# A new order of steps in a hand-written plan: the scaled up-projection weights used as they arrive, and steps moved between ScalarE, VectorE and GpSimd

## The chip, the cores and the metric

The kernel runs on one core of a Trainium2 chip. The metric is the device time of one execution in microseconds (us). Of three executions of the kernel before, the median was 151.3 us (148.43 to 152.84). A profiled execution took 148.72 us, and its span from the first to the last profiled instruction is 146.9 us. The engines are called by the names that the profile uses: PE is TensorE (PEld its weight loads), DVE is VectorE, ACT is ScalarE, POOL is GpSimd, and SP is SyncE, which here only issues transfers.

## The reference

A linear attention with a decaying state (batch 4, 8 heads, 768 positions, head size 48) is followed by a layer norm, a two-layer MLP with ReLU, and a residual:

```python
for t in range(S):
    cur = np.einsum('bhd,bhe->bhde', u[None] * kt, vt)
    y[:, :, t] = np.einsum('bhd,bhde->bhe', rt, state + cur)
    state = w[None, :, :, None] * state + np.einsum('bhd,bhe->bhde', kt, vt)
...
x = np.ascontiguousarray(attn_out.transpose(0, 2, 1, 3)).reshape(B, S, H * D)
...
xn = (x - mu) / np.sqrt(var + 1e-06) * g_ln
ch = np.maximum(xn @ w_ch1, 0.0) @ w_ch2
return (x + ch).astype(np.float32)
```

The model width is 8 x 48 = 384, the hidden width 1536.

## The kernel before

The 4 x 768 positions are cut into 24 chunks of 128, six to a sequence. Two chunks form a pair (12 pairs). For the MLP the chunks are put in 18 groups: groups 0 to 7 have one chunk each, 8 to 13 two, 14 to 17 one.

Every piece of work is a small function, a *step*, called by its name, a number and an engine letter: `v` for DVE, `s` for ACT, `g` for POOL, and `-` where the engine is fixed (PE for products, SP for transfers). The string `PLAN` (line 18 on) lists 755 such steps, and the last loop of the kernel calls them in that order. Nothing reorders them afterwards: on each engine the steps run in the order of the list, each held back only by waits for the data it reads and for the buffers it overwrites. So a step that waits holds all later steps of its engine. SP's transfers use eight completion semaphores in turn, so an issue there also waits for the landing of the transfer eight places before it.

The steps that matter here:

- `LK`, `LR2`/`LR`, `LV`: SP loads k, r and v of a chunk or a pair. `SK` and `SR2`/`SR` scale k and r by powers of the decay to bf16 (line 205). `TDk` turns a pair of scaled k by a transposing transfer (line 423); `TRr` turns r on PE and `TCr` copies it out of PSUM.
- `Q2` multiplies the turned k and r of a pair (line 205). `AT` forms the scores of a chunk on PE (line 544), `AM` masks them on DVE (line 553).
- `S` forms the chunk's own part of the state and the diagonal sums on PE (lines 460, 481); `ZU` and `ZD` carry the state on (ZD is a product by line 205), `CC2` copies the diagonal sums and `VB2` multiplies them by v (line 492).
- `Y` adds up the attention output on PE (lines 575, 583). `S` and `Y` share one PSUM bank, so `S` of a later pair waits until DVE's `X` (line 590) has read the `Y` before it. `X` writes the chunk's x and its row sums.
- `SQ` and `RS` make the norm's factor (RS on ACT in lines 613 and 614, on POOL in 616 and 619), `XN` the centred x in bf16. `LT` and `XT` (on PE and a copy), or from group 8 on the transposing transfer `LTD` (line 623), turn it.
- `LW1,n` loads a third of w1 as float; `SW,3n+kc` scales a piece of it into bf16 (line 342 on ACT, 344 on DVE, 346 on POOL). `IW2,n` loads a third of w2 (POOL's own transfers).
- `UP,16g+m` forms 512 columns of the hidden layer of group g on PE (line 646). For a group of one chunk, m = 0, 1, 2 uses the third 0, 1, 2 of w1. `RL` with the same number is the ReLU out of PSUM (662 on ACT, 664 on DVE). Two PSUM banks serve UP: an UP waits for the RL of the UP whose bank it takes.
- `DN,4i+d` adds a third of the down-projection of chunk i on PE (line 674), into a single bank; `OT` (line 730) multiplies by `RS` and adds x, and must have read the bank before the next chunk's `DN` starts. `STO` stores.
- `DU` are products with zeros that keep PE running in the first part (line 279).

Of the kernel before, what the change touches and what calls it, by code (L numbers as in the profile page):

```python
# [28 lines left out]
SW,1,s VB2,2,g AT,7,- AM,6,v LK,9,- Y,4,- RL,34,s UP,0,- IW2,1,g X,4,v UP,18,- RL,0,s AM,7,v IW2,2,g Y,5,- XN,4,s LT,3,- UP,32,-
RL,18,s RS,1,g LV,8,- X,5,v LT,4,- UP,33,- RL,32,s XT,3,v XN,5,g DU,512,- CV2,3,v LV,9,- UP,16,- RL,33,s XT,4,v SK,8,v S,6,-  # L30
DN,0,- SR2,4,v CC2,3,s RL,16,s UP,48,- SQ,5,s ZU,6,v UP,64,- VB2,3,v RL,48,s TRr,4,- SQ,3,s Y,6,- SK,9,g DN,1,- RS,3,s X,6,v
RL,64,s UP,66,- RS,0,g TDk,4,- SQ,2,s DN,2,- RS,2,g LT,5,- S,7,- OT,0,v RL,66,s UP,49,- XN,6,s XT,5,v UP,50,- RL,49,v TCr,4,s
LR2,6,- DN,4,- ZU,7,v DN,5,- UP,80,- ZD,7,v LK,10,- CV2,4,g RL,50,v Y,7,- RL,80,s X,7,v LV,13,- DN,6,- Q2,4,v XN,7,s UP,65,-
SQ,4,s OT,1,v LV,11,- AT,8,- SQ,6,s SR2,6,v AT,9,- DN,8,- RS,6,s LR2,5,- AM,8,v RS,4,s DN,9,- SQ,7,s LK,11,- S,8,- DN,10,-
ZU,8,v LV,10,- UP,82,- CC2,4,s OT,2,v VB2,4,g LK,12,- LT,6,- AM,9,v Y,8,- RL,82,s DN,12,- STO,0,- RL,65,s SK,10,g DN,13,- XT,6,v
LK,13,- X,8,v DN,14,- ZD,8,g LV,12,- S,9,- UP,96,- OT,3,v SK,11,g ZU,9,v UP,98,- RL,96,s SR2,5,v Y,9,- TDk,5,- SQ,8,s DN,16,-
CV2,5,v LT,7,- TRr,5,- SK,12,v DN,17,- X,9,v TCr,5,s RL,98,v LK,15,- UP,97,- XN,9,g LK,14,- XT,7,v ZD,9,g UP,81,- RL,97,s
LR2,7,- XN,8,s SK,13,g UP,112,- RL,81,s LTD,8,- DN,18,- RS,7,s Q2,5,v TRr,6,- OT,4,v UP,114,- SK,15,g TCr,6,s RL,112,v STO,1,-
S,10,- CV2,6,g DN,20,- CC2,5,s TDk,6,- RL,114,s SK,14,v AT,10,- RS,5,s AT,11,- ZU,10,v DN,21,- SR2,7,g AM,10,v UP,113,- STO,3,-
DN,22,- AM,11,v RL,113,s TDk,7,- Y,10,- VB2,5,g UP,129,- OT,5,v TRr,7,- RL,129,s LR,19,- UP,130,- ZD,10,g X,10,v UP,133,-  # L40
LV,14,- Q2,6,v RL,130,s DN,24,- TCr,7,v STO,2,- S,12,- DN,25,- CC2,6,s LV,15,- XN,10,s VB2,6,g ZU,12,v AT,12,- SQ,9,s AT,13,-
STO,5,- AM,12,v Y,11,- RL,133,s DN,26,- Q2,7,g LK,16,- X,11,v UP,128,- OT,6,v XN,11,s Y,12,- UP,131,- X,12,v LK,17,- DN,28,-
AM,13,v SR,19,g CV2,7,s S,13,- DN,29,- LTD,9,- ZU,13,v SQ,12,s DN,30,- ZD,13,g RL,128,s Y,13,- OT,7,v AT,15,- SQ,11,s LR2,8,-
AT,14,- X,13,v UP,132,- STO,4,- SK,17,g RL,131,v SQ,13,s LR,18,- S,14,- AM,15,v LV,17,- XN,13,s DN,32,- LV,16,- XN,12,s DN,33,-
ZU,14,v RL,132,s SK,16,v UP,144,- CC2,7,v AM,14,v LTD,10,- VB2,7,g UP,147,- RL,144,s DN,34,- SQ,10,s SR2,8,v TDk,8,- Y,14,-
RS,8,s UP,145,- RL,147,s OT,8,v UP,148,- TRr,8,- ZD,14,v TCr,8,s RL,145,v X,14,v RL,148,v DN,36,- LK,18,- DN,37,- CV2,8,v
XN,14,s S,15,- UP,149,- ZU,15,v LK,19,- UP,161,- ZD,15,g RL,149,v LV,18,- DN,38,- RL,161,s Q2,8,v STO,7,- Y,15,- LV,20,-
UP,146,- SK,18,g X,15,v STO,6,- AT,16,- RL,146,s AT,17,- XN,15,v LR,20,- UP,164,- RS,9,g OT,9,v LTD,11,- AM,17,v UP,160,-
RL,164,s RS,10,g DN,40,- RL,160,v S,16,- SK,19,v UP,163,- SR,18,v CC2,8,s TDk,9,- UP,165,- ZU,16,v RL,163,s AM,16,v DN,41,-
ZD,16,g RL,165,s DN,42,- VB2,8,g LR,21,- UP,162,- OT,10,v TDr,9,- Y,16,- RL,162,v DN,44,- X,16,v DN,45,- XN,16,g UP,176,-  # L50
LV,19,- SR,20,g DN,46,- RL,176,s STO,8,- Y,17,- OT,11,v UP,178,- LK,20,- X,17,v DN,48,- Q2,9,v LK,21,- UP,177,- XN,17,g SR,21,v
DN,49,- LTD,12,- RL,177,s RL,178,v DN,50,- CV2,9,v AT,19,- OT,12,v AT,18,- SK,20,g STO,9,- UP,180,- AM,18,v STO,11,- S,18,-
SK,21,g RL,180,s UP,181,- CC2,9,v ZU,18,v DN,52,- VB2,9,g AM,19,v RL,181,s STO,10,- UP,179,- SQ,16,s TDk,10,- DN,53,- RL,179,s
# [4 lines left out]
SR,22,v S,20,- RL,210,v UP,212,- TDr,11,- CC2,10,v DN,65,- SK,22,v VB2,10,g ZU,20,v DN,66,- Y,20,- TDk,11,- OT,16,v UP,209,-
X,20,v DN,68,- RL,209,s ZD,20,v STO,14,- S,21,- XN,20,g RL,212,v CV2,11,s DN,69,- LTD,14,- ZU,21,v SQ,20,s DN,70,- UP,213,-
RS,13,s OT,17,v STO,16,- UP,211,- STO,15,- Y,21,- RL,211,s DN,72,- X,21,v DN,73,- Q2,11,v SQ,21,s AT,23,- ZD,21,v RL,213,s  # L60
AT,22,- XN,21,v S,22,- LTD,15,- UP,224,- ZU,22,v AM,22,v DN,74,- ZD,22,g RL,224,s UP,226,- CC2,11,s RS,14,s OT,18,v VB2,11,g
# [721 lines left out]
```

## Time and profile before

| | us |
|---|---|
| three executions, median (lowest, highest) | 151.3 (148.43, 152.84) |
| profiled execution, its own time | 148.72 |
| its span | 146.9 |
| PE busy in the span | 140.5 |
| DVE, ACT, POOL busy | 110.7, 82.4, 71.8 |

The time lies 1.8 us above the span, for what comes before the first and after the last instruction. PE's busy time is modelled from pipelined matmuls, so it is read beside the idle time and the starts of the instructions. The granted TensorE clock was full in the whole span.

### The profile page before, as it was taken

The numbers are of one execution on the slowest core, as the hardware profiler recorded it, in microseconds if no ns is written. First come the engines' busy times: TensorE is split into PE (matmuls) and PEld (weight loads), VectorE is DVE, ScalarE is ACT, GpSimd is POOL, SyncE is SP. The second block draws the span as 40 slices with busy tenths as digits, with TensorE's granted clock in tenths as the row PEclk, the third lists the DMA queues.
The fourth block names the chain that finished last, engine by engine and source line by source line (L and its number), as shares of the span: only waits on it lengthen the run. The fifth ranks groups of instructions, "written<-read, shape, count | busy, mean of one in ns | idle before, by whom it ended". The sixth has DMA issues, their size and how long they took to land.

```text
span 146.9 us, 4689 instructions
## 1 busy us (share of the span) xinstructions
PE 140.5 (96%) x1943; PEld 111.1 (76%) x1943; DVE 110.7 (75%) x206; ACT 82.4 (56%) x181; POOL 71.8 (49%) x96
## 2 busy tenths in 40 slices
...
GB/s 114 285 251 265 182 373 161 287 230 213 220 90 235 199 229 153 219 204 262 218 192 196 178 216 170 185 206 225 204 103 198 175 119 173 84 49 115 11 97 110
DMA packets 85097, 27.18 MB, mean 185 GB/s; under 512 B 80338, under 2 KB 83540, under 8 KB 85076
## 3 DMA queue, kind: packets, MB, share of 16 engines
...
q8 instruction: 15, 0.25, 0.7%
...
HBM read 18.88 MB, written 4.72 MB: 161 GB/s over the span
## 4 chain that ended last, share of the span: by engine, by line
PE 78%; SPq 10%; DMA 6%; ACT 1%; issue 1%; DVE 1%; POOL 1%
PE hp L646 32%; PE o L674 31%; DMA w_f<-in_moe_w_ch_dram 6%; SPq L352 4%; PE at L544 3%; PE y L583 3%; SPq L374 2%; PE y L575 2%; PE y L481 2%; SPq L371 2%; PE at L400 2%; PE y L460 1%; SPq L377 1%; ACT w_sb L342 1%; SPq L218 1%
## 5 line engine op out<-in xcount | busy, mean ns | idle before, releaser
L646 PE MATMUL hp<-xT,w_sb 128*128 128x128 bf16 (+1 forms) x648 | 56.9, 238 | 0.7 <-ACT w_sb L342 0.7
L662 ACT ACTIVATE hT<-hp 128x512 bf16<-128x512 f32 x55 | 32.3, 594 | 41.4 <-PE hp L646 40.7
L674 PE MATMUL o<-w_sb,hT 128*128 128x384 bf16 x276 | 53.1, 326 | 0.5 <-DVE ot L730 0.5
L646 PEld LDWEIGHTS <-w_sb 128*128 128x128 bf16 x648 | 49.4, 114 | 4.8 <-ACT w_sb L342 1.2
L674 PEld LDWEIGHTS <-hT 128*128 128x128 bf16 x276 | 25.0, 97 | 12.6 <-issue 0.6
L553 DVE TENSOR_TENSOR A<-at,mask 128x1024 bf16<-128x1024 f32 x20 | 24.1, 1216 | 1.6 <-PE at L544 1.5
L730 DVE SCALAR_TENSOR_TENSOR ot<-o,rs,x 128x384 f32<-128x384 f32 x23 | 14.1, 615 | 12.8 <-PE o L674 7.0
L492 POOL TENSOR_TENSOR Vb<-vf,cc 128x768 f32<-128x768 f32 x11 | 16.5, 1499 | 14.7 <-ACT cc L200 7.8
L205 POOL TENSOR_TENSOR sk<-kf,Fk 128x384 bf16<-128x384 f32 x13 | 13.7, 1063 | 9.1 <-DMA kf<-in_k_dram 8.4
L597 ACT ACTIVATE sqj<-x,sm 128x384 bf16<-128x384 f32 x24 | 14.6, 610 | 2.2 <-DVE x L590 2.2
L205 POOL TENSOR_TENSOR Z<-ZS,WLZ 128x384 bf16<-128x384 f32 x8 | 8.0, 1001 | 15.3 <-DVE ZS L565 15.3
L590 DVE SCALAR_TENSOR_TENSOR x<-y,Vb 128x384 f32<-128x384 f32 x20 | 11.0, 552 | 4.8 <-PE y L583 3.7
L664 DVE TENSOR_SCALAR hT<-hp 128x512 bf16<-128x512 f32 x17 | 11.5, 682 | 3.3 <-PE hp L646 3.3
L279 PE MATMUL o<-warm 128*128 128x512 bf16 x33 | 11.3, 427 | 1.0 <-DVE warm L228 1.0
L200 ACT COPY trr<-at 128x512 bf16<-128x512 bf16 (+1 forms) x13 | 9.1, 762 | 5.1 <-PE at L400 5.1
L205 DVE TENSOR_TENSOR sr<-rf,Fr 128x768 bf16<-128x768 f32 (+1 forms) x11 | 9.3, 855 | 2.0 <-DMA rf<-in_r_dram 2.0
L205 POOL TENSOR_TENSOR sr<-rf,Fr 128x384 bf16<-128x384 f32 (+1 forms) x5 | 6.6, 1326 | 6.8 <-DMA rf<-in_r_dram 6.8
L205 DVE TENSOR_TENSOR q<-trk,trr 128x1024 bf16<-128x1024 bf16 x9 | 7.5, 833 | 1.6 <-DMA trk<-sk 1.3
L604 ACT ACTIVATE xn<-x,sm 128x384 bf16<-128x384 f32 x13 | 7.8, 610 | 1.3 <-DVE x L590 1.3
L606 POOL TENSOR_SCALAR xn<-x,sm 128x384 bf16<-128x384 f32 x8 | 4.9, 614 | 7.1 <-DVE x L590 7.0
L481 PE MATMUL y<-vv,sk 128*128 128x96 bf16 (+1 forms) x96 | 7.4, 205 | 0.0
L583 PE MATMUL y<-vv,A 128*128 128x48 bf16 x160 | 7.2, 183 | 0.0
...
## 6 DMA issues: line engine op xcount, KB each, us to landing
...
rf<-in_r_dram SPq DMA_DIRECT2D x9, 384.0 KB, 5.0
...
w_sb<-in_moe_w_ch_dram POOLq DMA_DIRECT2D x3, 384.0 KB, 6.5
...
kf<-in_k_dram SPq DMA_DIRECT2D x2, 384.0 KB, 4.6
```

What stands on the lines that cost most here:

```text
L205: engines[e].tensor_tensor(out=out, in0=in0, in1=in1, op=ALU.mult)
L279: nc.tensor.matmul(out=warm_ps[0][:].rearrange("p (a t) -> p a t", a=4), lhsT=warm[:], rhs=rhs, start=True, stop=True)
L492: engines[e].tensor_tensor(out=Vb2(g).rearrange("p (x h d) -> p x h d", x=2, h=H), in0=vals, in1=cc2(g)[:].unsqueeze(3).to_broadcast([P, 2 ...
L553: nc.vector.tensor_tensor(out=AA(i)[:].rearrange("p e q t -> p (e q) t"), in0=psum["at", i][:].rearrange("p e q t -> p (e q) t"), in1=mask ...
L583: nc.tensor.matmul(out=t[:, h * D : (h + 1) * D], lhsT=AA(i)[:, par, q, :], rhs=vv(i)[:, h, :], start=first, stop=True, skip_group_check=True,
L590: nc.vector.scalar_tensor_tensor(out=xx(i)[:], in0=psum["y", i][:, :C], scalar=1.0, in1=Vb(i), op0=ALU.mult, op1=ALU.add, accum_out=sm[i][:],)
L597: nc.scalar.activation(out=sqj[:], in_=xx(i)[:], func=ACT.Square, bias=sm[i][:], scale=-float(C), accum_out=sq[g][:, j : j + 1])
L646: nc.tensor.matmul(out=t[:, a * gw : (a + 1) * gw], lhsT=w1_sb[n][kc][:, fb::FB], rhs=xT(g)[:, :size, kc, :], start=(kc == 0), stop=(kc == ...
L662: nc.scalar.activation(out=o, in_=s, func=ACT.Relu)
L664: nc.vector.tensor_relu(out=o, in_=s)
L674: nc.tensor.matmul(out=psum["o", i][:, :C], lhsT=hT(g)[:, fk, j * P : (j + 1) * P], rhs=w2_sb[d][:, a, :], start=(fk == 0), stop=(fk == FK ...
L730: nc.vector.scalar_tensor_tensor(out=ot(i)[:], in0=psum["o", i][:, :C], scalar=rs[g][:, j : j + 1], in1=xx(i)[:], op0=ALU.mult, op1=ALU.add,)
```

## The change

Only `PLAN` changes, from the eighth line of its list on. The same 755 steps with the same numbers are called. SP's 110 steps stand in the same order. On PE some 38 of 255 steps stand elsewhere. 45 steps go to another engine, among them `SW,8` (ACT to POOL), `SW,0` (DVE to POOL), `RS,1` and `RS,2` (POOL to ACT), `Q2,3` and `VB2,4` (POOL to DVE), `Q2,5`, `SR2,5`, `SK,8`, `SK,12` (DVE to POOL), and 13 `RL` between ACT and DVE. Two lines of the table:

```diff
-XT,0,v Y2,3,- SW,7,s TCk,3,v X,2,v SW,8,s AT,5,- AT,4,- X,3,v XN,2,g DU,512,- UP,2,- AM,5,v XN,3,s IW2,0,g LV,7,- UP,1,- RL,2,s
+Y2,3,- TCk,3,v SW,7,s X,2,v X,3,v SW,6,s RS,1,s XN,2,s AT,5,- AT,4,- DU,512,- UP,1,- SW,8,g AM,5,v CV2,2,v UP,2,- LT,2,-
...
```

The first place is the start of the up-projection on PE. `w1_sb1` and `w1_sb2` are the scaled thirds 1 and 2 of w1; `hp` is the PSUM bank, `xT0` the turned chunk 0. Before:

```order
L279 MATMUL o_256<-warm_202 128x512
L646 LDWEIGHTS w1_sb2_0_232
L646 MATMUL hp_799<-xT0_129,w1_sb2_0_232 128x128
L646 LDWEIGHTS w1_sb2_1_233
L646 MATMUL hp_799<-xT0_129,w1_sb2_1_233 128x128
L646 LDWEIGHTS w1_sb2_2_234
L646 MATMUL hp_799<-xT0_129,w1_sb2_2_234 128x128
```

and in the changed kernel:

```order
L279 MATMUL o_256<-warm_202 128x512
L646 LDWEIGHTS w1_sb1_0_229
L646 MATMUL hp_800<-xT0_129,w1_sb1_0_229 128x128
L646 LDWEIGHTS w1_sb1_1_230
L646 MATMUL hp_800<-xT0_129,w1_sb1_1_230 128x128
L646 LDWEIGHTS w1_sb1_2_231
L646 MATMUL hp_800<-xT0_129,w1_sb1_2_231 128x128
```

`UP,1` (third 1) moves ahead of `UP,2` (third 2). On POOL the piece of third 2 with kc = 2 (`SW,8`) now follows `Q2,2`.

The second place is POOL after the last load of w2: `rs0` to `rs2` are `RS,0` to `RS,2`, `xn2` is `XN,5`, and `sk1_83` is written by `SK,9` before and by `SK,8` and `SK,9` after.

```order
 L349 DMA w2_sb2_237<-in_moe_w_ch2_dram 128x1536
-L616 TENSOR_SCALAR rs1_185<-sq1_166 128x1
-L619 TENSOR_TENSOR rs1_185<-rs1_185,expo_206 128x1
-L606 TENSOR_SCALAR xn2_128<-x5_119,sm5_146 128x384
-L205 TENSOR_TENSOR sk1_83<-kf0_69,Fk_213 128x8x48
 L616 TENSOR_SCALAR rs0_184<-sq0_165 128x1
 L619 TENSOR_TENSOR rs0_184<-rs0_184,expo_206 128x1
-L616 TENSOR_SCALAR rs2_186<-sq2_167 128x1
-L619 TENSOR_TENSOR rs2_186<-rs2_186,expo_206 128x1
+L205 TENSOR_TENSOR sk1_83<-kf0_69,Fk_213 128x8x48 x2
```

`RS,0` stood behind `SK,9` and now stands ahead of it.

The third place is POOL just after that: `sr2_87` is `SR2,5`, `sk2_84` is `SK,10` and `SK,11` (`SK,11` first after the change), `Z0` and `Z1` are `ZD,8` and `ZD,9`, the first `sk0_82` is `SK,12`, `q1_98` is `Q2,5`, and the last row is `SK,13`.

```order
 L202 CAST vv1_89<-vf4_81 128x768
-L492 TENSOR_TENSOR Vb0_112<-vf4_81,cc1_103 128x768
-L205 TENSOR_TENSOR sk2_84<-kf1_70,Fk_213 128x8x48
+L205 TENSOR_TENSOR sr2_87<-rf1_74,Fr2_209 128x16x48
+L205 TENSOR_TENSOR sk2_84<-kf1_70,Fk_213 128x8x48 x2
 L205 TENSOR_TENSOR Z0_105<-ZS2_111,WLZ_221 128x384
-L205 TENSOR_TENSOR sk2_84<-kf1_70,Fk_213 128x8x48
-L606 TENSOR_SCALAR xn2_128<-x9_123,sm9_150 128x384
+L205 TENSOR_TENSOR sk0_82<-kf2_71,Fk_213 128x8x48
 L205 TENSOR_TENSOR Z1_106<-ZS0_109,WLZ_221 128x384
+L205 TENSOR_TENSOR q1_98<-trk2_93,trr2_96 128x1024
 L205 TENSOR_TENSOR sk0_82<-kf2_71,Fk_213 128x8x48
```

`VB2,4` and `XN,9` leave POOL; `SR2,5`, `SK,12` and `Q2,5` come in, all ahead of `SK,13`, which `TDk,6` on SP waits for.

More of the change, by code (lines that the diff above doesn't have):

```diff
@@ L29 @@
[L29 to L53, printed above, removed]
@@ L58 @@
[L58 to L61, printed above, removed]
@@ new lines @@
+RL,34,s RL,18,s LV,8,- LV,9,- UP,0,- XN,4,s RL,0,s UP,32,- SK,9,g CV2,4,g TDk,4,- LR2,6,- LK,10,- LV,13,- LV,11,- LR2,5,-
+LK,11,- SR2,5,g SK,11,g SK,10,g LT,4,- UP,33,- DU,512,- Q2,3,v CV2,3,v XT,4,v RL,32,s RL,33,s UP,16,- UP,50,- RL,50,s DN,0,-
+S,6,- CC2,3,s SQ,5,s UP,48,- RL,48,s SQ,3,s RS,3,s XN,5,v SR2,4,v ZU,6,v TRr,4,- Y,6,- DN,1,- UP,66,- LT,5,- DN,2,- VB2,3,v
+X,6,v RL,16,v S,7,- UP,49,- OT,0,v XT,5,v RL,49,v ZU,7,v ZD,7,v DN,4,- DN,5,- SQ,2,s RL,66,s XN,6,s UP,64,- UP,80,- RL,64,s
+TCr,4,s Y,7,- DN,6,- X,7,v OT,1,v Q2,4,v UP,65,- AT,8,- AT,9,- AM,8,v LV,10,- LK,12,- STO,0,- LK,13,- LV,12,- TDk,5,- DN,8,-
```

46 lines of the change are left out of this document (35 added, 11 removed).

## The prediction

> **What bounds the kernel now.** First the stage from 45 to 90 us of the span (its length, then busy us of PE, PEld, DVE, ACT, POOL with their instructions, the clock granted, the DMA share, GB/s):
>
> ```profile
> 45.00:90.00 45.00, 45.00 (x609) 36.93 (x607) 41.22 (x73) 26.83 (x65) 25.39 (x24) 1.00 1.04 210
> ```
>
> From 45 us on PE has no idle time, at the full clock: there order can win nothing, only lose. What can be won lies earlier. The chain of waits shows where (start, length, engine, what is written and line):
>
> ```profile
> 24.71 0.86 ACT w_sb L342 x2
> 25.57 0.39 issue
> 25.96 0.71 ACT w_sb L342
> ...
> 40.81 0.61 ACT hT L662
> 41.42 0.20 POOL rs L616
> 41.69 0.56 POOL rs L619
> 42.28 0.63 DVE ot L730
> ```
>
> Two places: the scaling of w1 on ACT releases the first UP piece by piece, and RS,0 on POOL holds OT,0, for which DN,4 waits. PE's rows there, from the timeline (start, length, engine, line, what it writes from what, count, and in brackets the idle time before it and who ended that):
>
> ```profile
> 25.49 0.25 PE L646 MATMUL hp<-xT,w_sb 128*128 128x128 bf16 x1
> 26.11 0.25 PE L646 MATMUL hp<-xT,w_sb 128*128 128x128 bf16 x1 [0.37 <-ACT w_sb L342]
> 26.72 1.42 PE L646 MATMUL hp<-xT,w_sb 128*128 128x128 bf16 x22 [0.36 <-ACT w_sb L342]
> 27.98 0.33 PE L631 MATMUL at<-ident,xn 128*128 128x128 bf16 x3
> ...
> 40.95 1.50 PE L646 MATMUL hp<-xT,w_sb 128*128 128x128 bf16 x24
> 42.95 1.46 PE L674 MATMUL o<-w_sb,hT 128*128 128x384 bf16 x8 [0.49 <-DVE ot L730]
> ```
>
> From 26.72 to 27.98, 22 products take 1.26 us, so 0.057 us each and 0.68 for an UP of 12; a busy pair of UP (24) at 40.95 would end at 42.3, and DN,4 starts at 42.95: 0.65 lost. At 25.49 two products of 0.057 were spread over 1.23 us: 1.1 lost.
>
> **Front: UP,1 first, SW,8 on POOL.** The scaling of w1 in the timeline of POOL and ACT, with Q2,2 between (the second row), and the weight loads of Y,4:
>
> ```profile
> 22.83 0.97 POOL L346 TENSOR_SCALAR w_sb<-w_f,g_neg 128x512 bf16<-128x512 f32 x1 [1.04 <-DMA w_f<-in_moe_w_ch_dram]
> 23.77 2.12 POOL L205 TENSOR_TENSOR q<-trk,trr 128x1024 bf16<-128x1024 bf16 x1
> 24.71 1.95 ACT L342 ACTIVATE w_sb<-w_f,g_neg 128x512 bf16<-128x512 f32 x3 [1.32 <-DMA w_f<-in_moe_w_ch_dram]
> 29.86 1.34 ACT L342 ACTIVATE w_sb<-w_f,g_neg 128x512 bf16<-128x512 f32 x2
> 30.95 0.20 PEld L575 LDWEIGHTS <-trr 128*128 128x128 bf16 x4 [0.18 <-DVE Z L205]
> ```
>
> UP,1 needs SW,3 to SW,5, the last of them the POOL row that ends at 23.80; PE is free for it at 25.4, so it runs to 26.1. UP,2 needs SW,8, now behind Q2,2: 23.77 + 2.12 = 25.89, + 0.97 = 26.86, + 0.06 to PE (26.66 to 26.72 in the rows) = 26.92, 0.2 later than from ACT. UP,2's last ten products end at 27.49, where both UP ended at 27.98: gain 0.5.
>
> Behind it a new wait: UP,0 takes the bank of UP,34, whose RL stands on ACT behind XT,3, RL,17, SW,2 and SW,1. XT,3 waits for LT,3, which PE reaches at 29.1 (27.5 and 1.6 for LT,2, a DU, S,4 and UP,17, by the distances of their starts). So RL,17 ends near 30.4; + 1.34 + 0.6 for RL,34 (an RL on ACT, as at 40.81) = 32.3, while PE is ready at 32.0: 0.3 lost. In return SW,0 leaves DVE, where it sat ahead of ZU,4, for which Y,4 waited (last row): the 0.2 goes, and 0.1 comes for AT,6 and AT,7 being apart. CV2,2, new on DVE, puts AM,4 back by 0.8 to 28.5; LT,3 needs that bank at 29.1, so UP,17 covers it, and without this cover it would cost up to 0.8. After UP,33 the sum is 0.3 ahead.
>
> **RS,0 ahead of SK,9.** SK,9 on POOL, which waited for its load:
>
> ```profile
> 40.32 1.01 POOL L205 TENSOR_TENSOR sk<-kf,Fk 128x384 bf16<-128x384 f32 x1 [5.37 <-DMA kf<-in_k_dram]
> ```
>
> RS,0 stood behind it, at 41.42 (the chain above). It needs only SQ,0, which ran before SW,3 on ACT; after the change it follows the last w2 load on POOL and ends near 33.4, and OT,0 then waits for DN,2 alone, while PE runs S,7 and UP,49 (0.2 + 0.7), longer than one OT (0.62). The 0.65 goes. At UP,80 the sum is 0.95 ahead.
>
> **POOL at 50 to 62 us.** Here a new chain appears. The rows: the issue of the load LR2,5 on SP and the page's line on such loads (its last number is the median time to landing); SK,11 and an SR2 on POOL; the issues of TDk,5 and TDk,6, with the time to landing of all TDk; that of LTD,8, with the same for all LTD; and S,10 on PE.
>
> ```profile
> 46.33 1.86 SPq L374 DMA_DIRECT2D rf<-in_r_dram  x1
> rf<-in_r_dram SPq DMA_DIRECT2D x9, 384.0 KB, 5.0
> ```
>
> ```profile
> 53.40 1.01 POOL L205 TENSOR_TENSOR sk<-kf,Fk 128x384 bf16<-128x384 f32 x1
> 62.59 1.82 POOL L205 TENSOR_TENSOR sr<-rf,Fr 128x768 bf16<-128x768 f32 x1 [0.48 <-DMA rf<-in_r_dram]
> ```
>
> ```profile
> 54.44 1.29 SPq L423 DMA_TRANSPOSE trk<-sk  x1
> 61.08 1.28 SPq L423 DMA_TRANSPOSE trk<-sk  x1
> DMA to landing us min/median/max: 3.1/4.2/5.0
> ```
>
> ```profile
> 59.05 1.29 SPq L623 DMA_TRANSPOSE xT<-xn  x1
> DMA to landing us min/median/max: 2.3/2.9/4.2
> ```
>
> ```profile
> 60.49 0.34 PE L460 MATMUL y<-uwI,q 128*128 128x2 bf16 x8
> ```
>
> SR2,5 now heads POOL and waits for its load: 46.33 + 5.0 = 51.33. Then 1.82 for it and 1.0 each for SK,11 and SK,10: 55.15. So TDk,5, which needs both, is issued 0.75 later than 54.44, and all behind it on SP as much. ZD,8, SK,12 and ZD,9 take POOL to 58.15 (Y,9, which needs ZD,8 by way of ZU,9, now stands behind TRr,6, at 57.0 on PE against 56.8). Q2,5 waits there for TDk,5: 55.2 + 4.2 = 59.4, + 2.12 = 61.6. SK,13 comes next, to 62.6, and TDk,6, which needs it, is issued at 62.7 instead of 61.08.
>
> PE reaches S,10, which reads Q2,5, at 60.49 - 0.95 + 1.9 for AT,10, AT,11, DN,20 and UP,113, now ahead of it: 61.4. It starts at 61.7: 0.3 lost. UP,129, at 63.7 then, needs LTD,8: 59.8 + 2.9 to 4.2 = 62.7 to 64.0, a wait of 0 to 0.3, taken as 0.2. The sum falls to 0.45 ahead.
>
> **TDk,6, Q2,6, X,10, S,12.** X,10 and Q2,6 on DVE, S,12 on PE; then Q2,4 on DVE while POOL was idle, and ZD,10, which ran on POOL as Q2,6 began:
>
> ```profile
> 65.88 0.56 DVE L590 SCALAR_TENSOR_TENSOR x<-y,Vb 128x384 f32<-128x384 f32 x1 [0.86 <-POOL Vb L492]
> 66.36 0.99 DVE L205 TENSOR_TENSOR q<-trk,trr 128x1024 bf16<-128x1024 bf16 x1
> 67.58 0.34 PE L460 MATMUL y<-uwI,q 128*128 128x2 bf16 x8
> 45.97 0.69 DVE L205 TENSOR_TENSOR q<-trk,trr 128x1024 bf16<-128x1024 bf16 x1
> 65.80 1.01 POOL L205 TENSOR_TENSOR Z<-ZS,WLZ 128x384 bf16<-128x384 f32 x1
> ```
>
> Before, S,12 started 0.2 after Q2,6, with no slack, and X,10 had come first. Now X,10 stands behind Q2,6 on DVE, and S,12 needs X,10 to free its bank. TDk,6 lands at 62.7 + 4.2 = 66.9 (65.8 to 67.7 by the ends of its row); + 0.99 + 0.56 + 0.2 puts S,12 at 68.6. PE, with DN,25, AT,12 and AT,13 now in front, is there at 68.0. Wait 0.6, and the sum is **0.15 behind** (0.3 + 0.65 - 0.3 - 0.2 - 0.6); by the ends of that row the wait is 0 to 1.4. The masks, RL and POOL steps behind it are each one of the old rows long and follow PE, so the rest of the program keeps this distance. For Q2,6 I take 0.99, the row beside POOL work, as POOL will be busy then. The Trainium skill (SBUF — State Buffer, SBUF: two separate sides) says that DVE and GpSimd share a port pair which one holds for a whole instruction while the other is blocked. The trace agrees: 65.80 + 1.01 + 0.69 = 67.50, and that product ended at 67.35. By it Q2,6 would take 0.69 if it comes just before ZD,10 and 1.7 just behind, and the sum would be 0.15 ahead or 0.85 behind.
>
> **Costed at nothing.** The 13 RL that change engine and the POOL steps after 70 us lie beside a full PE, with DVE, ACT and POOL idle for 3.8, 18 and 20 of the 45 us in the first row above; if a DVE step there is late, the next X or OT is, and PE with it. The tightest place, by the issue of LTD,12, RL,177, and UP,194 that reads LTD,12:
>
> ```profile
> 97.12 1.21 SPq L623 DMA_TRANSPOSE xT<-xn  x1
> 97.66 0.60 ACT L662 ACTIVATE hT<-hp 128x512 bf16<-128x512 f32 x1 [2.40 <-PE hp L646]
> 103.92 1.47 PE L646 MATMUL hp<-xT,w_sb 128*128 128x256 bf16 x12
> ```
>
> LTD,12 now waits for XN,16 on ACT behind RL,177, whose UP is later by two DN (1.3): 97.66 + 1.3 + 0.6 + 0.6 = 100.2 instead of 97.12, landing at 103.1 by the 2.9 above, and UP,194 reads it at 103.92. The cover is 0.8; at 4.2 it is gone and 0.5 is lost. IW2,0 is issued one SW later (0.97), and DN,0, which reads it, stands one UP (0.68) later on PE; the other w2 loads are not later.
>
> **The rivals.**
> (a) Gain kept: TDk,6 lands in 3.1 (65.8), S,12 does not wait and 0.45 remains, 0.95 if S,10 and UP,129 find their inputs too: 147.8 to 148.3. For it: the transfers ahead of TDk,6 on SP are put back by 0.75 and it by 1.6, so less is in flight when it starts. Against: 4.2 is the median.
> (b) Slower: the POOL queue through SK,13. It decides once TDk,6 lands after 66.3 (68.0 less the 1.75 behind it); from there each us is one us. At 5.0, with 0.7 more for a blocked Q2,6, S,12 is at 70.1, a wait of 2.1, and the sum 1.65 behind: 150.4. For it: 2.12 for Q2,5 on POOL ahead of SK,13, where DVE needs 0.7 to 1.0.
> (c) The front does nothing: SW,8 late on POOL by another 0.5 takes away what UP,1 wins: 149.4. Against: POOL ran Q2,2 without idle time before it.
>
> **How the numbers follow.** All of this is against the profiled execution: 148.72 + 0.15 = 148.9. Three other executions had a median of 151.3, so the profiled one was among the fast; the middle of the four (148.43, 148.72, 151.3, 152.84) is 150.0, and with the 0.15 I predict **150.2** for the changed kernel. Chances: the forecast (within 0.5 of no change) 0.42, (a) 0.27, (b) 0.21, (c) 0.10. The largest terms are 0.95 ahead and 1.65 behind, under the 3.0 us that 2% makes (2% is about what a measurement of this kernel can tell from no change); only the spread of executions (3% between 148.43 and 152.84) reaches over it. So faster 0.08, same 0.83, slower 0.09. The range takes the fastest execution less the whole gain of (a), 147.5, and at the other end the slowest with the forecast's 0.15, 153.0; it leaves out (b) on the slowest executions and any still faster ones, some 2 in 10.
>
> **What would show it.** Right: PE runs UP without idle time from 25.4 to 26.1, then waits once for POOL's w_sb; DN,4 no longer waits for DVE's ot; Q2,5 on POOL ends near 61.6; PE idles near 61 and 68 us, before the products of line 460. Wrong: PE without idle time at 60 to 70 us (case a), idle time of over 1.5 us there (b), or DN,4 still late.

## The result, and the profile after

| | kernel before | changed kernel |
|---|---|---|
| first four executions, median (lowest, highest) | 150.88 (148.43, 152.84) | 153.86 (152.49, 155.33) |
| profiled execution, its span | 148.72, 146.9 | 153.6, 151.8 |
| ratio of the times, 95% interval | | 1.036 (1.029 to 1.043) |
| mean clock granted in the profiled execution | 1.000 | 0.989 |

In this series the changed kernel is slower, above the range that was predicted. All four of its executions had a mean granted clock of 0.989. A ratio leaves out executions that lie far above the fastest of their own kernel: in the later series these are most of those at a clock below 0.99, so their number stands beside each series, while the first ratio sets executions that all had the low clock against the kernel before.

Busy time by stage in the changed kernel: length of the stretch, then PE, PEld, DVE, ACT and POOL with their instructions, clock, DMA share, GB/s.

```profile
24.00:37.00 13.00, 13.00 (x265) 11.82 (x261) 10.19 (x21) 9.88 (x20) 8.25 (x11) 1.00 1.05 227
37.00:45.00 8.00, 4.62 (x43) 3.42 (x41) 3.84 (x6) 2.50 (x9) 1.98 (x2) 0.79 0.72 135
45.00:90.00 45.00, 43.99 (x586) 35.59 (x585) 38.39 (x66) 28.19 (x68) 28.75 (x25) 1.00 0.89 184
```

The first stage is full: the front does what the change says. From 37 to 45 us PE does 43 products where the kernel before did 111 (its row follows), and the clock falls to 0.79. From 45 us on PE, which had no idle time before, has 1.0 us of it. The row of the kernel before for 37 to 45 us:

```profile
37.00:45.00 8.00, 7.51 (x111) 6.38 (x108) 4.54 (x10) 5.56 (x14) 3.26 (x6) 1.00 0.77 149
```

The chain of waits of the changed kernel (start, length, what) leads to the loss at once:

```profile
25.97 2.05 SPq L358
28.02 0.04 issue
28.06 11.40 DMA rf<-in_r_dram
39.47 0.02 issue
39.49 0.97 DVE sr L205
40.46 0.05 issue
40.51 0.62 PE at L400 x8
```

It is the load `LR2,4`, then `SR2,4` on DVE, then `TRr,4`, which turns r on PE. None of the three stands in the prediction. PE's timeline at the first UP, at the stop, and at the two later waits:

```profile
25.38 1.50 PE L646 MATMUL hp<-xT,w_sb 128*128 128x128 bf16 x24
...
40.51 0.62 PE L400 MATMUL at<-ident,sr 128*128 128x128 bf16 x8 [3.38 <-DVE sr L205]
40.97 0.36 PE L583 MATMUL y<-vv,A 128*128 128x48 bf16 x8
41.17 1.22 PE L674 MATMUL o<-w_sb,hT 128*128 128x384 bf16 x4
42.18 1.49 PE L646 MATMUL hp<-xT,w_sb 128*128 128x128 bf16 x12
...
57.82 0.33 PE L481 MATMUL y<-vv,sk 128*128 128x96 bf16 x4 [0.46 <-DVE x L590]
70.77 0.81 PE L674 MATMUL o<-w_sb,hT 128*128 128x384 bf16 x4 [0.55 <-DVE ot L730]
```

`UP,1` and `UP,2` run as one piece of 24 products. After the stop, a DN of four products takes 1.22 us and an UP of twelve 1.49. For comparison, PE in the kernel before at the same steps:

```profile
37.99 0.61 PE L400 MATMUL at<-ident,sr 128*128 128x128 bf16 x8
38.44 0.36 PE L583 MATMUL y<-vv,A 128*128 128x48 bf16 x8
38.64 0.81 PE L674 MATMUL o<-w_sb,hT 128*128 128x384 bf16 x4
39.29 0.83 PE L646 MATMUL hp<-xT,w_sb 128*128 128x128 bf16 x12
```

There the same pieces took 0.81 and 0.83. From the start of `DN,1` to that of `UP,49` PE needed 2.31 us before (38.64 to 40.95) and 3.96 after (41.17 to 45.13): 1.65 more at the low clock.

So the account, at points where both kernels have done the same steps: the changed kernel is 1.04 ahead after `UP,0` and `UP,32`. The stop costs 3.38, the low clock 1.65, and the 0.49 of idle time ahead of `DN,4` is gone: 3.5 behind by the sum, 3.64 by the trace at `UP,64`. The two later waits and 0.2 of steps around them make 4.84, and the spans differ by 4.9.

Why was `LR2,4` late? It was issued at 28.06 to 29.45, ahead of the 29.62 to 30.32 of the kernel before, and landed at 39.47 instead of 35.64. By the completion events, 15 of its 16 shares (one per DMA engine) had ended at 35.13, and the last at 39.47, behind the last share of the w2 load `IW2,2` (39.20), which was issued 3.3 us later than `LR2,4`. One share in this stretch was late earlier too: the last share of `LK,8`, the load of k issued at 25.42, came at 32.18, 1.5 us after its fifteenth. POOL's rows say what became of those loads, first in the kernel before and then in the changed one:

```profile
30.57 1.48 POOL L492 TENSOR_TENSOR Vb<-vf,cc 128x768 f32<-128x768 f32 x1 [1.20 <-issue]
31.99 1.12 POOL L349 DMA_DIRECT2D w_sb<-in_moe_w_ch_dram  x2
```

```profile
28.69 1.47 POOL L492 TENSOR_TENSOR Vb<-vf,cc 128x768 f32<-128x768 f32 x1 [1.45 <-DVE cc L202]
30.11 0.59 POOL L349 DMA_DIRECT2D w_sb<-in_moe_w_ch_dram  x1
30.75 0.70 POOL L346 TENSOR_SCALAR w_sb<-w_f,g_neg 128x512 bf16<-128x512 f32 x1
31.39 0.57 POOL L349 DMA_DIRECT2D w_sb<-in_moe_w_ch_dram  x1
```

`VB2,2` waits for `CC2,2` on DVE. In the kernel before that stood behind `SW,0` there, which waited for its load of w1 (DVE's rows of the two):

```profile
29.87 0.49 DVE L344 TENSOR_SCALAR w_sb<-w_f,g_neg 128x512 bf16<-128x512 f32 x1 [1.16 <-DMA w_f<-in_moe_w_ch_dram]
30.27 0.17 DVE L202 COPY cc<-y 128x16 f32<-128x16 f32 x1
```

The change took `SW,0` away to POOL, `CC2,2` ran at 28.44, and so `VB2,2` runs 1.9 earlier, and behind it `IW2,1` 1.9 and `IW2,2` 1.2 earlier.

### The profile page after: what moved, and what is told of

Same layout as the page of the kernel before. It is cut to its first block, busy times and chain, and to the rows that moved or that the text cites. A ratio compares the mean times of both kernels' runs of the same rounds, so it can differ in the third digit from the quotient of the medians.

```text
span 151.8 us, 4683 instructions
## 1 busy us (share of the span) xinstructions
PE 142.5 (94%) x1943; PEld 112.4 (74%) x1943; DVE 110.2 (73%) x203; ACT 83.5 (55%) x186; POOL 74.6 (49%) x94
## 3 DMA queue, kind: packets, MB, share of 16 engines
q1 hardware_dynamic: 84642, 25.70, 76.1%
q0 software_dynamic: 432, 1.18, 4.2%
## 4 chain that ended last, share of the span: by engine, by line
PE 65%; DVE 15%; DMA 13%; SPq 3%; issue 2%; DVEq 0%
PE o L674 26%; PE hp L646 24%; DMA rf<-in_r_dram 10%; PE at L400 3%; DMA out_dram<-ot 2%; DVE A L525 2%; DVE sr L205 2%; PE at L544 2%; DVE sk L205 2%; PE y L583 2%; PE y L481 2%; DVE A L553 2%; PE y L575 2%; SPq L358 1%; DVE ot L730 1%
## 5 line engine op out<-in xcount | busy, mean ns | idle before, releaser
L662 ACT ACTIVATE hT<-hp 128x512 bf16<-128x512 f32 x58 | 33.7, 594 | 44.1 <-PE hp L646 38.0
L205 POOL TENSOR_TENSOR sk<-kf,Fk 128x384 bf16<-128x384 f32 x16 | 17.6, 1114 | 11.5 <-DMA kf<-in_k_dram 8.6
L492 POOL TENSOR_TENSOR Vb<-vf,cc 128x768 f32<-128x768 f32 x9 | 13.5, 1503 | 8.3 <-DVE cc L202 4.5
L205 POOL TENSOR_TENSOR sr<-rf,Fr 128x768 bf16<-128x768 f32 (+1 forms) x6 | 8.5, 1417 | 15.8 <-DMA rf<-in_r_dram 15.8
L664 DVE TENSOR_SCALAR hT<-hp 128x512 bf16<-128x512 f32 x14 | 9.5, 685 | 6.0 <-PE hp L646 6.0
L205 DVE TENSOR_TENSOR sr<-rf,Fr 128x384 bf16<-128x384 f32 (+1 forms) x10 | 9.7, 980 | 5.7 <-DMA rf<-in_r_dram 5.7
L200 ACT COPY trr<-at 128x512 bf16<-128x512 bf16 (+1 forms) x15 | 10.4, 761 | 3.1 <-PE at L400 3.1
L400 PE MATMUL at<-ident,sr 128*128 128x128 bf16 x72 | 5.7, 219 | 3.7 <-DVE sr L205 3.7
L400 PEld LDWEIGHTS <-sr 128*128 128x128 bf16 x72 | 4.3, 97 | 4.8 <-DVE sr L205 3.7
L565 DVE TENSOR_TENSOR ZS<-y,Z 128x384 f32<-128x384 f32 x12 | 6.6, 549 | 0.9 <-ACT cc L200 0.5
```

What stands on the lines that cost most here:

```text
L200: nc.scalar.copy(out=out, in_=in_)
L205: engines[e].tensor_tensor(out=out, in0=in0, in1=in1, op=ALU.mult)
L400: nc.tensor.transpose(out=psum[key][:, a, :], in_=flat[:, a, :], identity=ident[:])
L492: engines[e].tensor_tensor(out=Vb2(g).rearrange("p (x h d) -> p x h d", x=2, h=H), in0=vals, in1=cc2(g)[:].unsqueeze(3).to_broadcast([P, 2 ...
L662: nc.scalar.activation(out=o, in_=s, func=ACT.Relu)
```

## The experiments

Theory A: the w2 loads, issued earlier, go ahead of `LR2,4` on the DMA engines and hold it back. Theory B: SP's own loads, issued earlier, do it. Theory C: the loss is in the queues of POOL and DVE after 45 us.

All runs in one table, with what the one trace of each shows of `LR2,4` (us from the span's start); "low" counts all executions with a mean clock below 0.99. The kernel before had 26 of 90 such executions in the five series that stood beside these.

| run | LR2,4 issued | landed | IW2,1 and IW2,2 issued | PE idle at TRr,4 | low | median us |
|---|---|---|---|---|---|---|
| kernel before | 29.62–30.32 | 35.64 | 31.99, 32.58 | 0 | 26 of 90 | 149.62 |
| changed kernel, first series | 28.06–29.45 | 39.47 | 30.11, 31.39 | 3.38 | 4 of 4 | 153.86 |
| a2_again | 27.46–28.97 | 36.30 | 29.66, 30.94 | 0.49 | 4 of 10 | 150.94 |
| f3_after_third | 28.31–30.61 | 39.91 | 30.48, 31.75 | 3.46 | 4 of 6 | 153.58 |
| f1_r_last | 29.68–33.85 | 40.52 | 30.53, 31.81 | 3.58 | 3 of 4 | 155.11 |
| e2_before_w2_early | 28.10–29.56 | 38.45 | 28.91, 29.51 | 1.80 | 0 of 4 | 149.84 |
| e1_w2_later | 28.43–29.47 | 36.05 | 32.01, 32.64 | 0 | 0 of 4 | 151.15 |
| e6_w2_later_q2 | 29.78–32.08 | 41.06 | 31.64, 32.27 | 4.65 | 1 of 11 | 150.17 |
| e8_r_first_w2_later | 25.61–26.12 | 32.13 | 32.70, 33.33 | 0 | 0 of 6 | 151.27 |
| e10_undone_w2_later | 28.57–29.28 | 35.63 | 31.91, 32.54 | 0 | 0 of 12 | 149.74 |
| e3_r_first | 23.88–25.38 | 30.24 | 29.68, 30.95 | 0 | 5 of 10 | 153.33 |
| e9_pool_undone | 28.82–29.73 | 34.56 | 29.96, 31.23 | 0 | 3 of 12 | 148.54 |
| e4_pe_kept_busy | 28.38–29.09 | 36.69 | 30.28, 31.56 | 0 (filled with products) | 0 of 4 | 152.16 |
| f2_combined | 28.36–29.06 | 34.77 | 30.64, 32.13 | 0 | 1 of 6 | 149.91 |
| f4_sto_first | 28.43–29.14 | 34.93 | 31.42, 32.03 | 0 | 6 of 12 | 151.11 |
| e7_before_front | 28.13–29.72 | 34.67 | 31.60, 32.19 | 0 | 0 of 4 | 147.85 |
| e11_front_again | 28.12–29.64 | 35.76 | 31.08, 31.68 | 0 | 0 of 12 | 149.77 |

### The w2 loads later, and earlier in the kernel before

```diff
-VB2,2,g LV,7,- LR2,4,- LK,9,- IW2,1,g SW,0,g IW2,2,g RS,0,g
+VB2,2,g LV,7,- LR2,4,- LK,9,- SW,0,g RS,0,g IW2,1,g IW2,2,g
```

> The changed kernel with the loads IW2,1 and IW2,2 of w2 moved behind RS,0 on POOL, so that they are issued near 33 us of the span instead of 30.1 and 31.4. If they are what holds the last share of LR2,4 back (theory A), LR2,4 lands near 35.5 instead of 39.47, PE has no 3.4 us of idle time before the turning of r (line 400) and keeps the full clock: about 4.7 us less, near 149. The waits that the prediction gave to POOL's queue at 61 to 68 us (S,10, UP,129, S,12) may then show, together up to 1.1. If SP's own loads, issued earlier, hold LR2,4 back (theory B), it still lands near 39.5 and the time stays near 153.9. If the loss lies in POOL's queue after 50 us (theory C), the idle time at 37 goes but the time falls by less than 1 us.

The trace has no stop, and none of the four executions had a low clock, but the time was 151.15, a ratio of 1.020 (1.013 to 1.027): 2.7 less than the changed kernel, not 4.7. The other 2 us turn up mainly at 57 to 68 us (below); `DN,2` also waits 0.42 for the later `IW2,2`. In the kernel before:

```diff
-SW,1,s VB2,2,g ... UP,0,- IW2,1,g X,4,v ... AM,7,v IW2,2,g Y,5,-
+SW,1,s IW2,1,g IW2,2,g VB2,2,g ... UP,0,- X,4,v ... AM,7,v Y,5,-
```

> The kernel before with IW2,1 and IW2,2 moved ahead of VB2,2 on POOL, so that they are issued near 29.5 us instead of 32.0 and 32.6. Theory A: LR2,4, whose issue starts at 29.6 in the kernel before, gets its last share near 39 instead of 35.6, PE stops 2 to 3.5 us before the turning of r (line 400), and the time is 152.5 to 155 against some 150.9. Theory B: LR2,4 lands where it did and the time is within 0.5 of the kernel before.

Here both w2 loads went ahead of `LR2,4` on all 16 DMA engines: by the completion events the shares of `IW2,1` ended at 33.8 to 35.4, those of `IW2,2` 2.1 later, and those of `LR2,4` another 1.0 later. PE stopped at the same step:

```profile
39.49 0.62 PE L400 MATMUL at<-ident,sr 128*128 128x128 bf16 x8 [1.80 <-DVE sr L205]
```

The time rose by a ratio of 1.013 (1.002 to 1.023). `LR2,4` was issued 1.5 earlier than in the kernel before and landed 2.8 later, and only the w2 loads had moved: with theory B it would not have landed later. The stop was shorter than in the changed kernel, where the w2 loads were issued 1.2 and 1.9 later, and the clock stayed full. The median of 149.84 is less than the 152.5 expected: this stop of 1.80 at a full clock cost some 1.9 us (0.3 to 3.4 by the interval).

### Every execution lost; the changed kernel twice more

```diff
-LV,7,- LR2,4,- LK,9,- IW2,1,g
+LV,7,- LK,9,- LR2,4,- IW2,1,g
```

> The changed kernel with one pair of SP's loads exchanged: LR2,4 behind LK,9, so that its issue ends near 33, after both w2 loads (30.1 and 31.4), in every execution. The race theory: LR2,4 now loses always; it lands at 39 to 40.5, PE stands 3 us or more before the turning of r, and all executions have a clock of 0.99 or less and take 153 to 157 us, as the changed kernel in its first four executions. If LR2,4 has little to do with the slow executions, some of them stay at 149.6 and a full clock.

All four took 153.6 to 156.5, three at a low clock; the fourth, at a full clock, took 153.62. As `LR2,4` is itself issued up to 4.4 later here, this run shows what a late landing costs, and not that the w2 loads are what delays it. PE's timeline:

```profile
41.56 0.62 PE L400 MATMUL at<-ident,sr 128*128 128x128 bf16 x8 [3.58 <-DVE sr L205]
```

> The changed kernel once more, unchanged, on another day and perhaps another chip. If the late landing of LR2,4 belongs to its order of transfers (theory A), the mean granted clock is again below 1.00 in most of its executions and PE again stands 2 to 4 us before the turning of r; time near 153.9. If it was a chance of the profiled execution, LR2,4 lands near 36, as it did with products of zeros in the stop, and the clock stays at 1.00; time 149 to 151.

> The changed kernel unchanged, for more executions of it beside the kernel before on one chip. By the two series so far (four of four and four of ten with a clock of 0.99 or less) a third to two thirds of the executions have the low clock and take 152 to 157; the others take 149.2 to 150.4, a ratio of 1.00 to 1.01.

The first of these two profiles fell on an execution of 149.6, the second on one of 155.33:

```profile
37.34 0.62 PE L400 MATMUL at<-ident,sr 128*128 128x128 bf16 x8 [0.49 <-DVE sr L205]
```

```profile
40.95 1.03 PE L400 MATMUL at<-ident,sr 128*128 128x128 bf16 x8 [3.46 <-DVE sr L205]
```

One kernel, two outcomes, told apart by the landing of `LR2,4`: 36.30 and 39.91. A landing near 36 in a single trace, as in e1, therefore proves little without the clocks of its series. The last share of `LK,8` differed as well: 0.6 us behind its fifteenth in the first of these traces, 2.5 in the second. What makes a share late is not shown. Over its 20 executions the changed kernel had 12 at a low clock (152.5 to 156.9) and 8 at a full one (149.2 to 151.4, median 149.85), with nothing between. In these two later series its ratio was 1.004 (0.999 to 1.010) and 1.000 (0.990 to 1.010); the medians of all were 150.94 against 149.07 and 153.58 against 151.32, and 8 of 16 executions had the low clock where the kernel before, beside them, had 9 of 30.

### LR2,4 first, and both edits

```diff
-Q2,2,g ZU,3,v DU,1024,- LK,8,- XT,0,v ... LV,7,- LR2,4,- LK,9,-
+Q2,2,g ZU,3,v DU,1024,- LR2,4,- LK,8,- XT,0,v ... LV,7,- LK,9,-
```

> The changed kernel with the load LR2,4 ahead of LK,8 on SP; POOL's loads of w2 stay early. Theory A (a matter of order at one DMA engine): LR2,4 is issued some 4 us earlier, before any load of w2 but IW2,0, lands at 33 to 35, the stop of PE goes, and the time is near 149 to 150; LK,8 and SK,8 behind it are some 1.5 us later. Theory C: the stop goes, the time stays above 152.5.

`LR2,4` landed at 30.24, and five executions ran at 149.2 to 151.9 (ratio 1.008). But five had a low clock and took 154.8 to 157.5, which theory A in its first form does not allow.

> The changed kernel with both edits that were tried one by one: LR2,4 ahead of LK,8 on SP, and IW2,1 and IW2,2 behind RS,0 on POOL. With LR2,4 first alone, half of the executions still had a clock of 0.99 or less (154.8 to 157.5 us). If the stop comes from a race of POOL's w2 loads with whichever load of SP stands beside them in time (there LV,7, issued at 27.8 to 28.6, where LR2,4 was issued before) then moving both sides apart leaves none or one of the executions below 0.99, and the fast executions stay near 149.6, or 1 us above where DN,2 waits for IW2,2. If the low clock has nothing to do with w2, about half of the executions still show it.

None of six had a low clock. The time, 151.27 (ratio 1.018), is above the one expected, since the two late waits of e1 (below) are in this trace as well, with 0.86 and 0.96. So moving `LR2,4` alone does not take the low clock away, and moving the w2 loads behind `RS,0` does. That another load of SP takes its place in the race (`LV,7` was issued there at 27.79 to 28.57) fits, but no long execution of that kernel was traced. The four kernels with both w2 loads behind `RS,0` (e1, e6, e8, e10) had 1 low execution in 33, and the kernels with the change's own places (the changed kernel, e3, e9; f1 and e4, which force the delay, are left out) 20 in 42. That one execution in 33 was traced: SP was late (`LV,7` took from 26.13 to 29.73 to issue), so that `LR2,4` was issued beside the w2 loads after all, and PE stopped for 4.65.

### The clock

```diff
-SR2,4,v ZU,6,v TRr,4,- Y,6,- DN,1,-
+SR2,4,v ZU,6,v DX,7680,- TRr,4,- Y,6,- DN,1,-
```

> The changed kernel with 15 products with zeros (7680 columns, some 3.3 us) on PE just ahead of TRr,4, in the time in which it stood still; they write a bank whose content is overwritten. If the halved clock after the stop cost time of its own (1.3 us by the sum of the longer products), the clock stays at full in the slices from 37 to 45 us and the time is near 152.5. If the clock is a mere mark of the stop, or the halved products were hidden, the time stays at 153.9 or above.

The stretch from 37 to 45 us, then PE (line numbers are 8 higher in this kernel):

```profile
37.00:45.00 8.00, 8.00 (x82) 5.33 (x80) 4.74 (x10) 3.76 (x11) 1.82 (x2) 1.00 0.76 152
```

```profile
37.13 3.40 PE L287 MATMUL at<-warm 128*128 128x512 bf16 x15
40.36 0.61 PE L408 MATMUL at<-ident,sr 128*128 128x128 bf16 x8
40.81 0.36 PE L591 MATMUL y<-vv,A 128*128 128x48 bf16 x8
41.01 0.81 PE L682 MATMUL o<-w_sb,hT 128*128 128x384 bf16 x4
```

`TRr,4` starts at 40.36, as late as in the changed kernel (40.51), but the DN behind it takes 0.81 again, all four executions have a full clock, and the median is 152.16, 1.7 below the first series. `LR2,4` landed at 36.69 in this trace, so here the products themselves, and not the load, make `TRr,4` late; PE gets to it at the same time either way. So the low clock is a cost of its own beside the stop.

Its size is not always the 1.65 of the first profile. By the clock records of the traces the clock was at half for 3.41 us there and in f1, and for 6.83 in f3 and e6. From `TRr,4` to `UP,49` PE needed 2.96 in the kernel before, 4.62 and 4.63 in the first two, 5.63 and 5.59 in the others: 1.7 or 2.6 to 2.7 more. These two cases have mean clocks of 0.989, and of 0.975 and 0.978.

### The queues of DVE and POOL after 45 us

With the w2 loads later (e1), PE loses 0.87 and 1.44 at `UP,113` and `UP,129`:

```profile
63.41 0.83 PE L646 MATMUL hp<-xT,w_sb 128*128 128x128 bf16 x12 [0.87 <-DVE hT L664]
...
67.72 1.50 PE L646 MATMUL hp<-xT,w_sb 128*128 128x256 bf16 x12 [1.44 <-DMA xT<-xn]
```

DVE and POOL in the same kernel:

```profile
60.47 2.30 DVE L606 TENSOR_SCALAR xn<-x,sm 128x384 bf16<-128x384 f32 x1
62.68 0.68 DVE L664 TENSOR_SCALAR hT<-hp 128x512 bf16<-128x512 f32 x1
```

```profile
60.42 2.13 POOL L205 TENSOR_TENSOR q<-trk,trr 128x1024 bf16<-128x1024 bf16 x1 [0.44 <-DMA trk<-sk]
```

`XN,9` came 0.05 behind `Q2,5` and ended 0.2 after it. It held up `RL,114`, for which `UP,113` waits, and `LTD,8`, the transfer that `UP,129` reads.

```diff
-UP,112,- RL,114,v Q2,5,g SK,13,g
+UP,112,- RL,114,v Q2,5,v SK,13,g
```

> The changed kernel with IW2,1 and IW2,2 behind RS,0 and with Q2,5 on DVE, at its place behind RL,114, instead of POOL. With the loads alone moved, XN,9 took 2.29 us on DVE beside Q2,5 on POOL, and PE lost 0.87 before UP,113 and 1.44 before UP,129 (which waits for LTD,8, a transfer of XN,9). If Q2,5 on POOL is the cause (theory C for the part behind the stop), XN,9 takes 0.4 to 0.8, both waits go, and the time is about 2.0 less than with the loads alone: near 149.1. If not, the waits stay and the time is near 151.1.

Its ratio was 1.011 (1.007 to 1.016) against 1.020 (1.013 to 1.027): 1.3 us less, not 2.0, with intervals that overlap. In its trace `XN,9` takes 0.41. Neither wait is there, but this trace is that of the one execution at a low clock, and its stop of 4.65 us could have covered them:

```profile
67.59 0.41 DVE L606 TENSOR_SCALAR xn<-x,sm 128x384 bf16<-128x384 f32 x1
67.91 0.68 DVE L664 TENSOR_SCALAR hT<-hp 128x512 bf16<-128x512 f32 x1
68.51 0.68 DVE L205 TENSOR_TENSOR q<-trk,trr 128x1024 bf16<-128x1024 bf16 x1
```

In the changed kernel itself, without the stop (a2), the two waits of PE are others:

```profile
53.25 0.33 PE L481 MATMUL y<-vv,sk 128*128 128x96 bf16 x4 [0.85 <-DVE x L590]
66.38 0.81 PE L674 MATMUL o<-w_sb,hT 128*128 128x384 bf16 x4 [0.73 <-DVE ot L730]
```

Its DVE rows say why: `VB2,4`, which the change took from POOL, and `OT,5`.

```profile
50.35 2.17 DVE L492 TENSOR_TENSOR Vb<-vf,cc 128x768 f32<-128x768 f32 x1
52.63 0.56 DVE L590 SCALAR_TENSOR_TENSOR x<-y,Vb 128x384 f32<-128x384 f32 x1
...
65.71 0.62 DVE L730 SCALAR_TENSOR_TENSOR ot<-o,rs,x 128x384 f32<-128x384 f32 x1 [0.42 <-ACT hT L662]
```

`VB2,4` takes 0.95 in e1, beside an idle POOL; beside `SR2,5` and `SK,11` on POOL it takes 2.17 here, and `X,8` and `S,9` wait. `OT,5` reuses the buffer of `OT,1` (there are four), so it waits for the store `STO,1`, which landed at 65.59; the ReLU in the brackets is inferred, and `OT,5` uses nothing of it. In eleven more traces `OT,5` starts 0.12 or 0.13 after `STO,1` landed. That store stands behind `LTD,8` on SP, and `LTD,8` behind `XN,9`.

> The changed kernel with the exchange between DVE and POOL at 45 to 72 us undone: VB2,4, XN,9 and SR2,7 on POOL and SR2,5, SK,12 and Q2,5 on DVE again, in the order on POOL that the kernel before has. The w2 loads stay early. Where PE is not stopped at 37, the changed kernel was 1.2 ahead of the kernel before at UP,64 and 0.9 behind at the end: it lost 0.85 at S,9 (behind VB2,4 on DVE beside POOL's products), 0.73 at DN,24 (behind SR2,7 on DVE beside VB2,5 on POOL) and some 0.5 in small waits. If this exchange costs it (theory C), the executions without the low clock take 147.5 to 148.0, a ratio of 0.99 or 0.995; if the order of PE costs it, they stay at 149.6 (1.004). The low clock should stay as frequent as before, some 4 in 10.

> The same undone exchange with IW2,1 and IW2,2 behind RS,0 as well. The race theory: none or one of the executions below a clock of 0.99, and the others near 148.2 (0.4 for DN,2, which waits for IW2,2, above the run without the later loads). Without it: as frequent as there.

With the exchange undone (e9) the ratio was 0.999 (0.994 to 1.004) and the median at a full clock 148.35, against 1.004 in a2: a step of 0.5%, with intervals that overlap. With the loads later as well (e10) it was 1.005 (1.000 to 1.009) against 1.020 in e1, and no execution of twelve had a low clock. So with the w2 loads later the exchange cost some 2 us; with them early its cost is not clear of the noise. That bears out theory C for this part. Another wait stood in its place, 0.51 at `Y,8` in e9 and 0.93 in e10, behind `SR2,6` at the head of DVE and its load `LR2,6`.

### The front alone, and two combined versions

```diff
-SW,8,s AT,5,- AT,4,- X,3,v XN,2,g DU,512,- UP,2,- AM,5,v ... LV,7,- UP,1,- RL,2,s ... RL,1,s
+AT,5,- AT,4,- X,3,v DU,512,- UP,1,- SW,8,g XN,2,g UP,2,- AM,5,v ... LV,7,- RL,1,s RL,2,s
...
-SK,9,g DN,1,- RS,3,s X,6,v RL,64,s UP,66,- RS,0,g TDk,4,-
+RS,0,g SK,9,g DN,1,- RS,3,s X,6,v RL,64,s UP,66,- TDk,4,-
```

> The kernel before with three pieces of the change alone: UP,1 and RL,1 ahead of UP,2 and RL,2, SW,8 on POOL behind Q2,2, and RS,0 ahead of SK,9. The w2 loads keep their place behind VB2,2. Sum: 1.0 for the front (the lead that the changed kernel has behind its first two UP) and 0.65 for DN,4: 1.5 less than before if nothing eats it, so a ratio of 0.99. If VB2,2, and with it IW2,1, comes 1 us earlier too, LR2,4 is late (theory A), and PE stops 1 to 3 us: ratio 1.00 to 1.02.

> The kernel before with UP,1 first, SW,8 on POOL and RS,0 ahead of SK,9, once more, with more rounds: it was 0.99 of the kernel before in four executions of 147.6 to 148.1. LR2,4 landed at 34.67, before any share of IW2,1. If that order is as safe as it looked, the time is 147.6 to 148.1 again, at the full clock; as the loads stand where the kernel before has them, one execution in five may show the low clock, as there.

The first series gave 0.990 (0.984 to 0.996), the second, on another chip, 1.005 (1.000 to 1.010). The gain of this edit is therefore not shown. In the trace of the first, PE was 1.14 ahead after the first two UP, gave 0.60 of it back at `Y,4` (behind `SW,0` on DVE, which the whole change moves away), and with `DN,4` was 1.06 ahead to the end.

The first combined version is e9 with these further edits; the second puts `STO,1` just ahead of `LTD,8` instead and both w2 loads together behind `SW,0`:

```diff
-LK,9,- IW2,1,g SW,0,g IW2,2,g RS,0,g ... SR2,6,v ZU,8,v ... SK,11,g TDk,5,- AM,9,v X,8,v ... LTD,8,- STO,1,-
+LK,9,- SW,0,g IW2,1,g RS,0,g IW2,2,g ... ZU,8,v ... SK,11,g STO,1,- TDk,5,- AM,9,v SR2,6,v X,8,v ... LTD,8,-
```

> A version from what the runs show: the changed kernel with the exchange of DVE and POOL at 45 to 72 us undone; IW2,1 behind SW,0 and IW2,2 behind RS,0 (0.7 and 1.4 us later, where LR2,4 won in sixteen executions of another kernel); SR2,6 behind AM,9 on DVE, so that ZU,8 and CC2,4, and so Y,8, do not wait for LR2,6 (0.51 in the kernel without this edit); and STO,1 ahead of TDk,5 on SP, so that OT,5 and DN,24 do not wait for its landing (0.65 there). If these readings are right, both waits are gone from PE, and the time is 148.3 - 1.2 = 147.1 at the full clock, a ratio of 0.985 to 0.99, with one execution in ten or fewer at a clock of 0.99 or less.

> The combined version once more, without what turned against it: STO,1 stands just ahead of LTD,8 on SP (not ahead of TDk,5, where its issue of 1.57 us put TDk,5 and then LTD,8 back and PE waited 1.22 before UP,129), and IW2,1 and IW2,2 stand together behind SW,0. If Y,8 waited for LR2,6 and DN,24 for STO,1, and nothing takes their place, the time is 148.3 - 0.5 - 0.4 = 147.4 at the full clock, a ratio of 0.99; LTD,8 some 0.3 later may cost UP,129 up to 0.3. At most one execution in ten at a clock of 0.99 or less. If the ratio is 1.00, the change has no gain to keep.

Both waits went, as read, and the time did not: 1.001 (0.994 to 1.007) and 1.009 (1.003 to 1.016). PE, now earlier, waits for `LTD,8` instead. In f2:

```profile
65.22 1.50 PE L646 MATMUL hp<-xT,w_sb 128*128 128x256 bf16 x12 [1.22 <-DMA xT<-xn]
```

In f4 that wait is 1.07, and six of twelve executions had a low clock, though its w2 loads were issued at 31.42 and 32.03, close to those of the kernel before, and 2.3 us behind the end of the issue of `LR2,4`, where e1 and e10 have 2.5 and 2.6 and no low clock in 16. So the distance to `LR2,4` does not settle it alone; none of the six was traced. No version beat the kernel before in more than one series.

## Why the prediction was wrong, point by point

**The step that failed.** "IW2,0 is issued one SW later (0.97), and DN,0, which reads it, stands one UP (0.68) later on PE; the other w2 loads are not later", costed at nothing. In the trace `IW2,0` is not later (26.43 against 26.41), and "not later" asked only half the question: the other two were 1.9 and 1.2 earlier, and what earlier transfers collide with was left out. The failed term is this one: put at nothing, it measured 3.38 of idle time and 1.65 of low clock in the first profile. The load they collided with had little slack. From its landing to the start of `TRr,4` at least 1.04 pass (39.47 to 40.51), and PE turned r at 37.99 in the kernel before, so `LR2,4`, which landed at 35.64, had 1.3 us. In the changed kernel PE was ready for it at 37.13, so its own lead had left 0.45. e2 shows the collision in the kernel before; with the w2 loads behind `RS,0` (e1, e6, e8, e10) one execution in 33 had the low clock. f1 shows the price of a late landing alone.

**Front.** Its size was too small, 0.3 ahead against 1.04 in the trace. `SW,8` ran on POOL in 0.68 us and ended at 25.90, where 26.86 was forecast from a row of 0.97, and PE did not wait for it. Part of that was luck: `Q2,2` ahead of it began at 22.93 in this execution, not at 23.77. In e10, with the same steps up to there, it began at 23.92, `SW,8` ended at 26.73, and PE did wait, 0.24. The wait of 0.3 at `UP,0` did not occur.

**DN,4.** Right: its idle time is gone in every trace of the changed kernel.

**POOL's chain.** `Q2,5` ended at 63.69 in the first profile (61.6 predicted), at 59.73 in a2. `S,10` and `S,12`, put at 0.3 and 0.6, did not wait. `UP,129`, put at 0.2, lost 1.44 in e1, 1.22 in f2 and nothing in the changed kernel. The chain was there, but it reached PE by other links: `Q2,5` beside `XN,9`, `VB2,4` beside `SR2,5`, and `STO,1` ahead of `OT,5`. In a2, where PE stopped for only 0.49, the trace ended 0.86 behind; the sum said 0.15. The size is near, through the wrong steps.

The port rule that the prediction weighed fits these lengths. `XN,9` started in e1 just after `Q2,5` and ended at 62.77, 0.22 after the end of `Q2,5` at 62.55, so most of its 2.30 was waiting for POOL's instruction. The Trainium skill (SBUF — State Buffer, SBUF: two separate sides) says that whichever starts first gets the pair for the whole instruction; these rows agree. The prediction applied it to `Q2,6` alone.

**Rivals and range.** None of the rivals had a stop at 37 us. The range of 147.5 to 153.0 holds the eight executions of the changed kernel at a full clock and one of the twelve others. The prediction took the spread of executions (148.43 to 152.84) as given. That spread may in part be the same thing as the loss: 26 of 90 executions of the kernel before had the low clock, 12 of 20 of the changed one. Whether those 26 too are a late `LR2,4` stays open, as none of them was traced; e3 and f4 say that `LR2,4` may not be the only load that can lose.
